# A fused attention and two-layer MLP kernel: the clamp of the weights' top byte moves from GpSimd to ScalarE, in a new order

## Chip, cores and metric

The kernel runs on one core of a Trainium2 chip. The metric is the device time in microseconds (us) of one execution.

## What is computed

The reference chains three parts. The first is an attention over 2 batches, 8 heads, 768 tokens and a head size of 64, in which a key counts only where it falls into the same hash bucket as the query:

```
mask = q_bucket[:, :, :, None] == k_bucket[:, :, None, :]
scores = np.where(mask, scale * np.matmul(q, k.transpose(0, 1, 3, 2)), -1e9)
attn = np.exp(scores - max) / (sum + 1e-09)
```

Its output, 1536 tokens of 512 numbers, goes through a first MLP: `h = x @ w_in` (512 to 2048), `g = h * tanh(softplus(h))`, `g @ w_out` (2048 to 512). Then comes a second one: `h = x @ w_in` (512 to 1024), `h * softmax(h)`, a layer norm with the gain `g_ln`, and `@ w_out` (1024 to 512). The weights arrive as 64-bit floats; every product is taken as a sum of three products of parts (high by high, high by low, low by high).

## The kernel before

The program is one long list of steps over five engines. `program_order` declares every step with its engine, cost and what it reads and writes; `Order.run` turns that into one order per engine, from the costs in `COST` and from offsets in `PHASE`, a table of numbers that sets how urgent each kind of step is. Each engine then works through its own list in order: a step that waits holds back all behind it on that engine.

Three stretches follow one another in time. **Attention**: 96 tiles of 128 queries by 768 keys. For each, TensorE makes the scores (L1180), VectorE the row maximum (L1187), ScalarE the exponential (L1196); the result is split into two fp16 parts (ScalarE L1207 and GpSimd L1229, or through TensorE, L1215 to L1224) and weighed with `v` on TensorE (L1247 to L1249). **First MLP**: 48 units, each one block of 512 tokens by 128 hidden numbers. In a unit TensorE does 12 matmuls of 512 columns up (`up`, L800 to L802) and 12 down (`down_high`, `down_low`, L856 to L861). Between the two stands the activation, `mish`, eleven steps `a0` to `a10`: ScalarE exp (L816), VectorE (L818, L820, L822), ScalarE logarithm (L824) and exp (L826), VectorE (L828, L830), GpSimd product `n` (L834), ScalarE high part `gh` (L839), GpSimd low part `gl` (L842). The units share two PSUM banks `h`: a unit's bank is free for the second unit after it once L830 is done. **Second MLP**: 12 tiles of 128 tokens (L905 to L975), without GpSimd.

The weights come in 48 chunks of 128 by 512 doubles. `chunk` declares and `w_step` issues the conversion of a chunk to fp32 in six steps. The load puts the chunk into a tile `wr`, shifted by one byte, so that the sign and the top seven exponent bits of each double stand in a byte of their own (`top`) and the next 32 bits in a word (`low`). Step `w0` (ScalarE, L693) writes `top` times 2^27 as a float to a PSUM bank `wq`; `w1` (GpSimd, L696) clamps `top` to plus or minus 56 into the tile `wf`; `w2` (VectorE, L698) takes the clamped byte times 2^27 from `wq` and stores it as an integer; `w3` (VectorE, L700) joins it with the shifted `low`; `w5` (ScalarE, L707 or L709) and `w6` (GpSimd L713, for the last eight chunks VectorE L715) make the two parts that the matmuls read. Tiles `wr` and `wf` have two buffers each, `wq` has one bank. Four chunks are converted during the attention, the others while the first MLP runs.

```
        if j == 0:
            nc.scalar.activation(q, top, AF.Copy, scale=TOP)
        elif j == 1:
            t.append(p.tile([128, 512], F32, tag="wf", name="wf"))
            nc.gpsimd.tensor_scalar(t[1].bitcast(I8)[:, 0:512], top, -EXP_GAP, EXP_GAP, op0=ALU.max, op1=ALU.min)
        elif j == 2:
            nc.vector.scalar_tensor_tensor(q.bitcast(I32), t[1].bitcast(I8)[:, 0:512], -TOP, q, op0=ALU.mult, op1=ALU.add)
```

Of the kernel before, what the change touches and what calls it, by code (L numbers as in the profile page):

```python
# [9 lines left out]
F32 = mybir.dt.float32  # L10
F32R = mybir.dt.float32r
F16 = mybir.dt.float16
I8 = mybir.dt.int8
I32 = mybir.dt.int32
AF = mybir.ActivationFunctionType
ALU = mybir.AluOpType
# [11 lines left out]
TOP = 2.0 ** 27  # L28
EXP_GAP = 56


PHASE = dict(
    score=3.18, max=2.53, bias=-167.78, exp=-11.41, hi=43.25, lo=-29.73, tdma=-251.87, tr0=9.20, thi0=-31.01,
    tlo0=7.90, tr1=10.26, thi1=22.25, tlo1=-118.98, weigh=17.76, norm0=-27.63, norm1=-69.89, norm2=-117.62,
    load=57.26, vload=-17.69, split0=185.96, rest0=-39.72, split1=19.36, rest1=6.02, turn=-2.32, evac=-159.74,
    copy=-179.38, bits0=-325.74, bits1=4.40, sign=-9.22, bdma=2.32, vmax=104.27, vs0=-114.44, vs1=-42.67,
    vs2=-72.72, vs3=-18.05, vs4=-74.05, vs5=12.38, vs6=-32.00, vs7=-32.58, vs8=14.06, vh=32.22, vl=-142.30,
    first=-210.30, turn_=42.29, evac_=59.56, copy_=-124.42, bits_=64.90, sign_=163.79, bdma_=142.14,
    vload_=-52.66, vmax_=346.44, vs_=-185.69, vh_=90.08, vl_=-136.17, second=28.07, wload=168.86, w0=36.13,
    w1=191.13, w2=126.06, w3=-34.77, w4=-53.41, w5=6.07, w6=124.56, wpace=-53.43, wat=182.43, wlate=-729.27,  # L40
    turngap=0.64, x0_=-3.53, x1_=-148.94, x2_=153.79, load_=10.62, const0=-101.54, begin0=25.07, vs8_=220.89,
    outlag=-1.85, up=-43.62, a0=23.99, a1=11.15, a2=58.10, a3=153.65, a4=-268.52, a5=-90.91, a6=3.61,
    a7=-137.25, a8=69.62, a9=-156.92, a10=83.71, da=59.12, db=-9.71, ky0=52.83, ky1=17.06, x0=20.21, x1=21.53,
    x2=-180.26, sy0=-146.63, sy1=221.79, u2=-66.64, n0=-239.67, n1=241.84, n2=-76.83, n3=-225.79, n4=-25.00,
    n5=74.29, n6=-371.20, n7=108.91, n8=115.67, n9=-108.58, n10=-44.93, n11=-50.71, n12=-49.24, n13=144.69,
    t2=-55.28, l0=-163.64, l1=43.42, d2=146.11, ot=22.49, od=-41.99, wloadL=-187.89, w0L=8.05, w1L=49.78,
    w2L=117.28, w3L=-140.95, w4L=-342.97, w5L=-28.48, w6L=-114.27, begin1=-124.80, begin2=17.00, begin3=-13.01,
    const1=161.30, const3=171.44, load0_=4.64,
)


# [1 line left out]
    score=0.7, max=0.865, bias=0.14, exp=0.878, hiA=0.733, hiD=0.469, lo=1.596, tr=0.325, thi=0.371, tlo=0.469,  # L53
    weigh=0.533, norm0=0.075, norm1=0.106, norm2=0.469, split=0.915, rest=1.79, turn=0.5,
    evacA=0.691, evacD=0.865, bits=0.69, sign=0.985, vmax=0.87, vs0=0.11, vs1=0.2, vs2=0.11,
    vs=0.07, vs8=0.884, vh=0.733, firstA=0.413, firstD=0.469, w0=0.52, w1=0.6, w2=0.602,
    w3=0.602, w5=0.52, w6P=1.225, w6D=0.663, x0=0.434, x1=0.478, x2=0.602,
    up=0.68, a0=0.478, a1=0.335, a2=0.602, a3=0.613, a4=0.52, a9=0.52, a10=1.225, da=0.453, db=0.2265,
    sy0=0.52, sy1=0.602, u2=1.36, n0=1.131, n1=1.091, n2=0.069, n3=0.075, n4=1.196, n5=0.069, n6=1.133,
    n7=0.188, n8=0.094, n9=0.069, n10=0.13, n11=0.069, n12=0.069, n13=0.723, t2=0.87, d2=2.72,  # L60
)
WIRE = dict(load=1.3, load0=0.65, vload=1.3, wload=1.65, copy=1.08, bdma=0.2, tdma=1.6,
            od=0.728, const0=0.185, const1=0.028, const2=0.028, const3=0.448)
# [206 lines left out]
def program_order(pairs, tiles, routes, evac, chunks, due, rings, stores, slack, queues=(), pooled=0,  # L270
# [6 lines left out]
    A, V, G, T = "Activation", "DVE", "Pool", "PE"  # L277

    def dma(key, base, name, reads=(), writes=(), slot=0, behind=()):
        fast = key[0] in ("load", "load0", "vload", "wload", "const", "od")  # L280
        op(key, A if key[0] in queues else "SP", 0.54 if fast else 0.8 if key[0] == "bdma" else 0.625, base, name, reads, writes, slot, behind)
# [117 lines left out]
    def chunk(i, base, slot, reads):  # L399
        late = i >= chunks  # L400
        wr, wf = ((x + "2" * late, i) for x in ("wr", "wf"))
        q = "L" if late else ""
        dma(("wload", i), base, "wload" + q, [("wg", i - 1)] + reads, [wr], 0, (("bdma", 0, (0,), 0, 1),))
        wq = ("wq", i)
        steps = [(A, "w0", [wr], [wq]), (G, "w1", [wr], [wf]), (V, "w2", [wf, wq], [wq]), (V, "w3", [wr, wq], [wf]),
                 (A, "w5", [wf], [slot]), (V if plan[i][0][0] == "out2" else G, "w6", [wf], [slot])]
        for j, (e, nm, r, w) in enumerate(steps):
            cost = COST.get(nm + e[0], COST.get(nm))
            op(("w", i, j), e, cost, base, nm + q, r, w + ([("wg", i)] if j == 0 else []), 0,
               [("w", i - 1, j)] if nm == "w5" and i else [])  # L410
# [160 lines left out]
def lsh_attention_moe_kernel(  # L571
# [14 lines left out]
    evac="AAAA",  # L586
# [23 lines left out]
    nc = tc.nc  # L610
# [17 lines left out]
    const = ctx.enter_context(tc.tile_pool(name="const", bufs=1, side="left"))  # L628
# [9 lines left out]
    ones = const.tile([1, 128], F32, name="ones")  # L638
    eps = const.tile([128, 1], F32, name="eps")
    two = const.tile([128, 1], F32, name="two")  # L640
    pcol = const.tile([128, NC], F32, name="pcol")


# [15 lines left out]
    def job(i):  # L659
        (kind, j, *half), slot, _ = plan[i]  # L660
        if kind == "in":
            return chunk_cols(w1_in, j * 128), None
        if kind == "out":
            return chunk_rows(w1_out, j * 128, 0), None
        if kind == "in2":
            return chunk_rows(w2_in, j * 128, half[0] * 512), None
        return chunk_rows(w2_out, j * 128, 0), glt[:, j:j + 1]
# [18 lines left out]
    def w_step(i, j):  # L686
        src, scale = job(i)
        p, t = pools["wr", i >= nconv], raw_w[i]
        top = t[0].bitcast(I8)[:, 8:4104].rearrange("p (n a) -> p n a", a=8)[:, :, 0]
        low = t[0][:, 0:1024].rearrange("p (n a) -> p n a", a=2)[:, :, 1]  # L690
        q = bank("wq", i)
        if j == 0:
            nc.scalar.activation(q, top, AF.Copy, scale=TOP)  # L693
        elif j == 1:
            t.append(p.tile([128, 512], F32, tag="wf", name="wf"))
            nc.gpsimd.tensor_scalar(t[1].bitcast(I8)[:, 0:512], top, -EXP_GAP, EXP_GAP, op0=ALU.max, op1=ALU.min)  # L696
        elif j == 2:
            nc.vector.scalar_tensor_tensor(q.bitcast(I32), t[1].bitcast(I8)[:, 0:512], -TOP, q, op0=ALU.mult, op1=ALU.add)  # L698
        elif j == 3:
            nc.vector.scalar_tensor_tensor(t[1].bitcast(I32), low, 5, q.bitcast(I32), op0=ALU.logical_shift_right,  # L700
                                           op1=ALU.bitwise_or)
        elif j == 4:
            tags = ("xt", "xt") if plan[i][1][0] == "xs" else ("wh", "wl")
            parts[plan[i][0]] = tuple(w_pool(i).tile([128, 512], F32R, tag=x, name="w") for x in tags)
            hi = parts[plan[i][0]][0]
            if scale is None:
                nc.scalar.activation(hi, t[1], AF.Copy)  # L707
            else:
                nc.scalar.activation(hi, t[1], AF.Copy, scale=scale)  # L709
        else:  # L710
            hi, lo = parts[plan[i][0]]
            if scale is None:
                nc.gpsimd.tensor_tensor(lo, t[1], hi.bitcast(F32), op=ALU.subtract)  # L713
            else:
                nc.vector.scalar_tensor_tensor(lo, t[1], scale, hi.bitcast(F32), op0=ALU.mult, op1=ALU.subtract)  # L715
            raw_w.pop(i)
# [36 lines left out]
    def bank(*tok):  # L753
        return banks[:, order.place[tok]]
# [9 lines left out]
    def step(name, make):  # L764

        def run(*key):
            if key[-1] == 0:
                gen[name, key[:-1]] = make(*key[:-1])
            next(gen[name, key[:-1]])
        return run  # L770
# [521 lines left out]
    nc.gpsimd.memset(ones, 1.0)  # L1292
    nc.gpsimd.memset(eps, 1e-6)
    nc.gpsimd.memset(two, 2.0)
    for c in range(NC):
        nc.gpsimd.memset(pcol[:, c:c + 1], 1e-9 if routes[c] in "Dd" else 1e-9 * PSCALE)
    for w in v_t:
# [16 lines left out]
        load=load_qk, load0=load_first, split=qk_split, rest=qk_rest, const=const_in, begin=begin,  # L1314
        first=lambda i, h, o: (first_high, first_low)[i](h, o),
        turn=qk_turn, evac=qk_evac, copy=qk_copy, bits=bits, sign=signs, bdma=bits_in, vload=load_v,
        vmax=v_max, vs=step("vs", v_scale), vh=v_high, vl=v_low, score=scores, max=row_max,
        bias=row_bias, exp=exps, hi=hi_part, lo=lo_part, tdma=turn_dma, tr=turn_half, thi=half_high,
# [35 lines left out]
```

## Time and profile before

| | |
|---|---|
| median of 3 runs (lowest to highest) | 688.05 us (686.13 to 688.23) |
| the profiled execution's own time | 687.81 us |
| its span, first to last instruction | 686.0 us, 12209 instructions |
| TensorE busy | 639.6 us (93%) |
| VectorE busy | 486.8 us (71%) |
| ScalarE busy | 439.3 us (64%) |
| GpSimd busy | 431.0 us (63%) |

The profile is of one execution. PE is TensorE's matmul, PEld its weight load, DVE is VectorE, ACT ScalarE, POOL GpSimd; an engine name with a q is its queue. The share of a whole span mixes stretches with different limits: GpSimd is near full until about 520 us and has nothing to do in the last 140 us. A matmul's end is modelled and overlaps the start of the next, so TensorE's busy time hides short gaps; its pace is read from the starts.

### The profile page before, as it was taken

How to read it: one execution, taken by the hardware profiler on the slowest of the kernel's cores; microseconds unless marked ns; L12 is line 12 of the kernel's file. 1: busy time of each engine (PE TensorE's matmuls, PEld its weight loads, DVE VectorE, ACT ScalarE, POOL GpSimd, SP SyncE). 2: the span in 40 equal slices, each digit the busy share in tenths (PEclk: the TensorE clock that was granted, in tenths of full speed). 3: DMA queues.
4: the chain of work that ended last, by engine and by line, in shares of the span. 5: the costliest groups of instructions: out<-in, count | busy, mean ns of one | idle time of the engine just before them, and what ended most of it. 6: DMA issues, size and time to landing. Idle time of an engine off the chain costs nothing.

```text
span 686.0 us, 12209 instructions
## 1 busy us (share of the span) xinstructions
PE 639.6 (93%) x4520; PEld 515.3 (75%) x4520; DVE 486.8 (71%) x1017; ACT 439.3 (64%) x718; POOL 431.0 (63%) x309
## 2 busy tenths in 40 slices
PE   6899998999999998989988899999999999999997
PEld 4678776888988865667666667787767888888886
DVE  3867868778989777868677678968867685634540
ACT  6788999999999855655454556654555443532441
POOL 4886986876767887989989988848885200000000
PEclk9889999999999999999999999999999999999999
DMA  5979999899988932322222232301200000000011
GB/s 149 250 146 169 221 149 171 182 183 177 155 161 175 199 120 82 103 71 84 92 72 82 92 104 82 106 17 62 93 31 1 0 1 1 31 17 15 31 47 46
DMA packets 125148, 68.11 MB, mean 99 GB/s; under 512 B 103584, under 2 KB 118048, under 8 KB 125088
## 3 DMA queue, kind: packets, MB, share of 16 engines
q1 hardware_dynamic: 125088, 67.33, 42.6%
q8 instruction: 35, 0.57, 0.4%
q14 instruction: 25, 0.20, 0.1%
HBM read 34.68 MB, written 3.15 MB: 55 GB/s over the span
## 4 chain that ended last, share of the span: by engine, by line
PE 39%; POOL 28%; DVE 10%; issue 8%; ACT 8%; DMA 6%; SPq 1%; POOLq 0%; ACTq 0%; DVEq 0%
POOL wf L696 7%; POOL n L834 7%; POOL gl L842 6%; POOL w L713 6%; PE banks L1180 4%; PE banks L906 3%; PE banks L905 3%; PE banks L909 3%; PE banks L971 3%; PE banks L970 3%; PE banks L969 3%; DVE mx L1187 3%; DMA store<-store 3%; ACT gh L839 3%; DMA B<-bits 2%
## 5 line engine op out<-in xcount | busy, mean ns | idle before, releaser
L1229 POOL TENSOR_TENSOR store<-store 128x768 f16<-128x768 f32 x64 | 104.7, 1652 | 28.9 <-ACT store L1207 21.0
L1187 DVE TENSOR_REDUCE mx<-banks 128x1 f32<-128x768 f32 x96 | 90.5, 950 | 26.8 <-PE banks L1180 22.1
L1196 ACT ACTIVATE store<-banks,mx 128x768 f32<-128x768 f32 x96 | 93.7, 992 | 7.9 <-DVE mx L1192 4.4
L696 POOL TENSOR_SCALAR wf<-wr 128x512 int8<-128x512 int8 x48 | 96.2, 2005 | 0.8 <-DMA wr<-in_moe_w_out_dram 0.5
L842 POOL TENSOR_TENSOR gl<-n,gh 128x512 fp32r<-128x512 f32 x48 | 62.4, 1300 | 48.8 <-ACT gh L839 31.9
L800 PE MATMUL banks<-xh,w 128*128 128x512 f32 x192 | 78.9, 411 | 10.7 <-DVE a L830 9.4
L861 PE MATMUL banks<-gl,w 128*128 128x512 f32 x192 | 75.6, 406 | 7.7 <-POOL gl L842 7.4
L802 PE MATMUL banks<-xh,w 128*128 128x512 f32 x192 | 76.6, 399 | 0.2
L856 PE MATMUL banks<-gh,w 128*128 128x512 f32 x192 | 76.4, 398 | 0.3 <-ACT banks L826 0.3
L801 PE MATMUL banks<-xl,w 128*128 128x512 f32 x192 | 76.0, 396 | 0.0
L857 PE MATMUL banks<-gh,w 128*128 128x512 f32 x192 | 75.9, 395 | 0.0
L834 POOL TENSOR_TENSOR n<-c,a 128x512 f32<-128x512 f32 x48 | 62.5, 1302 | 18.2 <-DVE a L830 13.4
L839 ACT ACTIVATE gh<-n 128x512 fp32r<-128x512 f32 x48 | 30.2, 629 | 58.5 <-POOL n L834 58.2
L1180 PE MATMUL banks<-A,A 128*128 128x384 f32 x192 | 58.0, 383 | 7.5 <-ACT store L1196 6.1
L824 ACT ACTIVATE a<-n,two 128x512 f32<-128x512 f32 x48 | 34.5, 719 | 44.7 <-DVE n L820 44.7
L1247 PE MATMUL banks<-v,store 128*128 128x65 f16 x576 | 60.7, 194 | 1.8 <-DMA store<-store 1.4
L1248 PE MATMUL banks<-v,store 128*128 128x64 f16 x576 | 60.4, 195 | 0.0
L1249 PE MATMUL banks<-v,store 128*128 128x65 f16 x576 | 60.1, 192 | 0.0
L1247 PEld LDWEIGHTS <-store 128*128 128x128 f16 x576 | 53.1, 97 | 7.3 <-issue 4.6
L800 PEld LDWEIGHTS banks<-xh,w 128*128 128x128 f32 x192 | 36.4, 190 | 28.2 <-DVE a L830 17.5
L1248 PEld LDWEIGHTS <-store 128*128 128x128 f16 x576 | 53.6, 98 | 1.2 <-issue 0.7
L713 POOL TENSOR_TENSOR w<-wf,w 128x512 fp32r<-128x512 f32 x40 | 51.7, 1293 | 3.9 <-ACT w L707 3.9
(122 smaller groups left out, 1715.2 us busy)
## 6 DMA issues: line engine op xcount, KB each, us to landing
wr<-in_moe_w_in_dram SPq DMA_DIRECT2D x24, 512.0 KB
wr<-in_moe_w_out_dram SPq DMA_DIRECT2D x24, 512.0 KB
vr<-in_v_dram SPq DMA_DIRECT2D x8, 384.0 KB
B<-A SPq DMA_DIRECT2D x16, 192.0 KB
out_dram<-ot SPq DMA_DIRECT2D x12, 256.0 KB
q<-in_q_dram SPq DMA_DIRECT2D x7, 384.0 KB
k<-in_k_dram SPq DMA_DIRECT2D x7, 384.0 KB
B<-bits SPq DMA_DIRECT2D x32, 36.0 KB
```

The lines of the kernel that those rows point to most:

```text
L696: nc.gpsimd.tensor_scalar(t[1].bitcast(I8)[:, 0:512], top, -EXP_GAP, EXP_GAP, op0=ALU.max, op1=ALU.min)
L713: nc.gpsimd.tensor_tensor(lo, t[1], hi.bitcast(F32), op=ALU.subtract)
L800: nc.tensor.matmul(h, lhsT=wh[:, ks], rhs=xh, start=(kk == 0), stop=False)
L802: nc.tensor.matmul(h, lhsT=wl[:, ks], rhs=xh, start=False, stop=(kk == KD - 1))
L834: nc.gpsimd.tensor_tensor(g, t("c"), t("a"), op=ALU.mult)
L842: (nc.vector if late == "V" else nc.gpsimd).tensor_tensor(g_t[u][1], g, t("gh").bitcast(F32), op=ALU.subtract)
L1180: nc.tensor.matmul(s[:, half, 0:NH], lhsT=opnd[nm, p, j, 0][:, cc], rhs=opnd[nm, p, j, 1][:, hs], start=(i == 0), stop=(i == 1),)
L1187: nc.vector.reduce_max(m[:, 1:2], two_banks("s", t)[:, :, 0:NH], axis=AX.XY, negate=True)
L1196: nc.scalar.activation(kept("e", t).rearrange("p (a n) -> p a n", a=2), two_banks("s", t)[:, :, 0:NH], AF.Exp, bias=m[:, 3:4], scale=m[:, ...
L1229: nc.gpsimd.tensor_tensor(p16[:, 1], kept("e", t), p16[:, 0], op=ALU.subtract)
L1247: nc.tensor.matmul(o, lhsT=pt[:, 0, kc, :], rhs=vh, start=(kc == 0), stop=False)
L1248: nc.tensor.matmul(o[:, 0:D], lhsT=pt[:, 0, kc, :], rhs=vl, start=False, stop=False)
```

## The change

Step `w1` leaves GpSimd. `w0` now writes max(top * 2^27 - 56 * 2^27, 0) and `w1`, on ScalarE, max(-top * 2^27 - 56 * 2^27, 0); `w2` subtracts the second from the first. The difference is what the byte less its clamped value gave. The constant -56 * 2^27 stands in a new one-column tile `gap`, which the two read as their bias and which GpSimd fills at the start. The table `PHASE` has all its numbers changed and two costs are set to 0.65, so the order is made anew on every engine.

```
 PHASE = dict(
-    score=3.18, max=2.53, bias=-167.78, exp=-11.41, hi=43.25, lo=-29.73, tdma=-251.87, tr0=9.20, thi0=-31.01,
...
+    score=3.69, max=0.87, bias=-330.22, exp=12.74, hi=253.86, lo=-96.05, tdma=-189.01, tr0=9.77, thi0=14.69,
...
-    vs=0.07, vs8=0.884, vh=0.733, firstA=0.413, firstD=0.469, w0=0.52, w1=0.6, w2=0.602,
+    vs=0.07, vs8=0.884, vh=0.733, firstA=0.413, firstD=0.469, w0=0.65, w1=0.65, w2=0.602,
...
-        steps = [(A, "w0", [wr], [wq]), (G, "w1", [wr], [wf]), (V, "w2", [wf, wq], [wq]), (V, "w3", [wr, wq], [wf]),
+        steps = [(A, "w0", [wr], [wq]), (A, "w1", [wr], [wf]), (V, "w2", [wf, wq], [wq]), (V, "w3", [wr, wq], [wf]),
...
+    gap = const.tile([128, 1], F32, name="gap")
...
-            nc.scalar.activation(q, top, AF.Copy, scale=TOP)
+            nc.scalar.activation(q, top, AF.Relu, scale=TOP, bias=gap)
...
-            nc.gpsimd.tensor_scalar(t[1].bitcast(I8)[:, 0:512], top, -EXP_GAP, EXP_GAP, op0=ALU.max, op1=ALU.min)
+            nc.scalar.activation(t[1], top, AF.Relu, scale=-TOP, bias=gap)
...
-            nc.vector.scalar_tensor_tensor(q.bitcast(I32), t[1].bitcast(I8)[:, 0:512], -TOP, q, op0=ALU.mult, op1=ALU.add)
+            nc.vector.scalar_tensor_tensor(q.bitcast(I32), t[1], -1.0, q, op0=ALU.mult, op1=ALU.add)
...
+    nc.gpsimd.memset(gap, -EXP_GAP * TOP)
```

How the order moves is shown at three places. In the changed kernel the lines are one or two further down. The first place is GpSimd's list around the seventeenth unit of the first MLP: `n` and `gl` are the unit's two steps, `w` is step `w6` and `wf` step `w1` of a chunk. Before:

```order
L834 TENSOR_TENSOR n_4949<-c_4960,a_4937 128x512
L842 TENSOR_TENSOR gl_5007<-n_4949,gh_5000 128x512
L713 TENSOR_TENSOR w_5015<-wf_4983,w_5014 128x512
L696 TENSOR_SCALAR wf_5033<-wr_4979 128x512
L834 TENSOR_TENSOR n_4998<-c_5012,a_4987 128x512
```

And with the change:

```order
L835 TENSOR_TENSOR n_4943<-c_4957,a_4935 128x512
L843 TENSOR_TENSOR gl_5011<-n_4943,gh_5001 128x512
L714 TENSOR_TENSOR w_5009<-wf_4980,w_5008 128x512
L835 TENSOR_TENSOR n_4988<-c_5006,a_4976 128x512
L714 TENSOR_TENSOR w_5058<-wf_5030,w_5057 128x512
L843 TENSOR_TENSOR gl_5074<-n_4988,gh_5065 128x512
```

The step between one unit's `w6` and the next unit's `n` is gone, and nothing takes its place.

The second place is ScalarE's list in the same unit, from its first exponential (L816, then L817): L693 and L694 are `w0`, L697 is the new `w1`, L707 and L708 are `w5`. Before:

```order
L816 ACTIVATE banks_75<-banks_75 128x512
L839 ACTIVATE gh_4951<-n_4898 128x512
L824 ACTIVATE a_4937<-n_4949,two_70 128x512
L707 ACTIVATE w_4965<-wf_4934 128x512
L826 ACTIVATE banks_75<-a_4937 128x512
L693 ACTIVATE banks_75<-wr_4929 128x512
L816 ACTIVATE banks_75<-banks_75 128x512
```

And with the change, one unit on:

```order
L817 ACTIVATE banks_76<-banks_76 128x512
L694 ACTIVATE banks_76<-wr_4927,gap_71 128x512
L697 ACTIVATE wf_4980<-wr_4927,gap_71 128x512
L825 ACTIVATE a_4976<-n_4988,two_70 128x512
L840 ACTIVATE gh_5001<-n_4943 128x512
L708 ACTIVATE w_5008<-wf_4980 128x512
L827 ACTIVATE banks_76<-a_4976 128x512
```

The pair `w0`, `w1` now stands between the unit's first exponential and its logarithm, where `gh` of the unit before stood; `gh` follows the logarithm.

The third place is ScalarE in the attention, at the first of the four chunks converted there (L1196 and L1197 are the exponentials of the score tiles). Before:

```order
L693 ACTIVATE banks_75<-wr_339 128x512
L1196 ACTIVATE store_105<-banks_75,mx3_100 128x768
L1219 ACTIVATE store_105<-banks_75 128x384
L1207 ACTIVATE store_105<-store_105 128x768
L1196 ACTIVATE store_105<-banks_75,mx4_101 128x768
```

And with the change:

```order
L697 ACTIVATE wf_628<-wr_342,gap_71 128x512
L694 ACTIVATE banks_76<-wr_342,gap_71 128x512
L1197 ACTIVATE store_106<-banks_76,mx3_101 128x768
L1208 ACTIVATE store_106<-store_106 128x768
L1197 ACTIVATE store_106<-banks_76,mx4_102 128x768
```

Both steps stand ahead of the next exponential. The whole ScalarE list of the changed kernel holds one table load, at its start, as before.

## Rows read from the trace of the kernel before

**Rows 1.** The chain that ended last, shares of the span by engine and line.

```profile
PE 39%; POOL 28%; DVE 10%; issue 8%; ACT 8%; DMA 6%; SPq 1%; POOLq 0%; ACTq 0%; DVEq 0%
POOL wf L696 7%; POOL n L834 7%; POOL gl L842 6%; POOL w L713 6%; PE banks L1180 4%; PE banks L906 3%; PE banks L905 3%; PE banks L909 3%; PE banks L971 3%; PE banks L970 3%; PE banks L969 3%; DVE mx L1187 3%; DMA store<-store 3%; ACT gh L839 3%; DMA B<-bits 2%
```

**Rows 2.** The chain in order of time, one unit: start us, us, what.

```profile
328.18 1.95 POOL wf L696
330.13 1.28 POOL n L834
...
331.43 0.64 ACT gh L839
...
332.14 1.30 POOL gl L842
333.44 1.14 POOL w L713
...
334.64 1.96 POOL wf L696
```

**Rows 3.** Groups of GpSimd instructions: busy us, mean ns, idle before, releasers.

```profile
L696 POOL TENSOR_SCALAR wf<-wr 128x512 int8<-128x512 int8 x48 | 96.2, 2005 | 0.8 <-DMA wr<-in_moe_w_out_dram 0.5
L842 POOL TENSOR_TENSOR gl<-n,gh 128x512 fp32r<-128x512 f32 x48 | 62.4, 1300 | 48.8 <-ACT gh L839 31.9 <-PE banks L861 15.8 <-PE banks L801 1.1
```

**Rows 4.** Waits, longest first: us in total, times, longest us.

```profile
ACT gh L839 <- POOL n L834: 58.2, 33, 3.8
ACT a L824 <- DVE n L820: 44.7, 31, 3.5
```

**Rows 5.** TensorE's matmuls in order of time, first and last of twelve: start, us.

```profile
303.64 0.40 PE L800 MATMUL banks<-xh,w 128*128 128x512 f32 x1
...
306.20 0.40 PE L802 MATMUL banks<-xh,w 128*128 128x512 f32 x1
```

**Rows 6.** Stretches: length, busy us (count) of PE, PEld, DVE, ACT, POOL; PEclk, DMA, GB/s.

```profile
60.00:223.00 163.00, 152.98 (x2038) 133.37 (x2037) 137.06 (x366) 156.16 (x222) 126.42 (x83) 1.00 0.93 174
223.00:262.00 39.00, 34.37 (x352) 27.05 (x350) 28.99 (x54) 26.49 (x46) 33.15 (x23) 1.00 0.66 142
262.00:375.00 113.00, 102.96 (x411) 75.98 (x411) 82.89 (x129) 62.66 (x111) 100.20 (x71) 0.98 0.28 88
375.00:435.00 60.00, 56.35 (x233) 42.57 (x232) 47.27 (x75) 34.98 (x62) 53.60 (x37) 1.00 0.27 88
435.00:520.00 85.00, 81.64 (x343) 63.37 (x342) 65.06 (x102) 46.02 (x80) 65.53 (x45) 1.00 0.17 56
520.00:533.00 13.00, 13.00 (x58) 10.57 (x57) 10.33 (x16) 6.82 (x13) 6.39 (x5) 1.00 0.01 2
```

**Rows 7.** Line L696 alone in three of these stretches: length, POOL busy (count).

```profile
262.00:375.00 113.00, 34.81 (x18) 0.98 0.28 88
375.00:435.00 60.00, 20.87 (x11) 1.00 0.27 88
435.00:520.00 85.00, 20.92 (x10) 1.00 0.17 56
```

**Rows 8.** Groups of ScalarE instructions: busy us, mean ns, idle before, releasers.

```profile
L693 ACT ACTIVATE banks<-wr 128x512 f32<-128x512 int8 x48 | 30.0, 624 | 4.3 <-DVE a L830 1.9 <-DMA wr<-in_moe_w_out_dram 1.4 <-DMA wr<-in_moe_w_in_dram 0.6
L824 ACT ACTIVATE a<-n,two 128x512 f32<-128x512 f32 x48 | 34.5, 719 | 44.7 <-DVE n L820 44.7
L707 ACT ACTIVATE w<-wf 128x512 fp32r<-128x512 f32 x40 | 25.0, 624 | 17.2 <-DVE wf L700 17.1
L709 ACT ACTIVATE w<-wf,glt 128x512 fp32r<-128x512 f32 x8 | 5.7, 711 | 0.0
L627 ACT ACT_TABLE_LOAD x1 | 1.3, 1283 | 0.7 <-PEq L1338 0.7
```

**Rows 9.** Groups of VectorE instructions: busy us, mean ns, idle before, releasers.

```profile
L698 DVE SCALAR_TENSOR_TENSOR banks<-wf,banks 128x512 int32<-128x512 int8 x48 | 33.2, 692 | 27.6 <-POOL wf L696 27.4 <-ACT banks L693 0.2
L828 DVE SCALAR_TENSOR_TENSOR a<-n,banks 128x512 f32<-128x512 f32 x48 | 32.9, 685 | 26.0 <-ACT banks L826 25.3
```

More of the change, by code (lines that the diff above doesn't have):

```diff
@@ L32 @@
 PHASE = dict(
-    score=3.18, max=2.53, bias=-167.78, exp=-11.41, hi=43.25, lo=-29.73, tdma=-251.87, tr0=9.20, thi0=-31.01,
[L34 to L47, printed above, removed]
@@ L48 @@
-    const1=161.30, const3=171.44, load0_=4.64,
+    score=3.69, max=0.87, bias=-330.22, exp=12.74, hi=253.86, lo=-96.05, tdma=-189.01, tr0=9.77, thi0=14.69,
+    tlo0=4.19, tr1=10.11, thi1=75.90, tlo1=-207.08, weigh=17.00, norm0=-35.41, norm1=-226.56, norm2=-78.50,
+    load=129.70, vload=75.26, split0=453.42, rest0=274.23, split1=209.91, rest1=322.17, turn=-1.39,
+    evac=-101.44, copy=-173.09, bits0=-324.87, bits1=5.03, sign=-117.83, bdma=135.73, vmax=30.34, vs0=-33.79,
+    vs1=-146.49, vs2=-188.08, vs3=-25.17, vs4=-176.05, vs5=207.64, vs6=-228.20, vs7=-38.10, vs8=-29.32,
@@ new lines @@
+    vh=171.54, vl=-118.08, first=-636.50, turn_=106.45, evac_=-17.59, copy_=-135.91, bits_=109.21, sign_=186.80,
+    bdma_=302.63, vload_=-136.00, vmax_=-58.57, vs_=-137.35, vh_=486.24, vl_=-22.15, second=-6.75, wload=356.57,
+    w0=122.15, w1=233.00, w2=453.40, w3=-132.54, w4=-118.88, w5=26.88, w6=-124.83, wpace=-43.83, wat=169.36,
+    wlate=-944.98, turngap=0.47, x0_=-22.09, x1_=-199.05, x2_=165.20, load_=-4.58, const0=-117.46,
+    begin0=-133.70, vs8_=320.02, outlag=44.69, up=-206.71, a0=-25.55, a1=33.80, a2=79.27, a3=227.95, a4=-374.57,
@@ new lines @@
+    a5=-161.92, a6=-9.47, a7=-120.59, a8=-84.30, a9=-164.37, a10=363.32, da=69.39, db=-368.55, ky0=14.03,
+    ky1=88.45, x0=-105.44, x1=-102.23, x2=-93.30, sy0=57.14, sy1=387.61, u2=256.06, n0=-140.91, n1=257.67,
+    n2=-53.84, n3=-206.26, n4=34.90, n5=68.87, n6=-476.27, n7=90.14, n8=-151.97, n9=-30.78, n10=-42.23,
+    n11=26.26, n12=-13.08, n13=464.05, t2=65.16, l0=-65.93, l1=-63.15, d2=309.12, ot=-137.74, od=-190.53,
+    wloadL=-427.87, w0L=-54.06, w1L=-32.31, w2L=76.07, w3L=-275.48, w4L=-365.85, w5L=-91.93, w6L=-68.34,
@@ L49 @@
+    begin1=-314.58, begin2=47.74, begin3=100.37, const1=147.93, const3=246.73, load0_=16.27,
 )
```

## Prediction

> **What bounds the kernel now.** I read the chain that ended last first. By line, its largest single piece is the clamp L696 with 7% of the span, next to the three other GpSimd steps of the first MLP, and GpSimd makes 28% of the whole chain [rows 1]. In order of time one sees why: from 328.18 to 334.64 us the chain runs clamp, `n`, `gh`, `gl`, `w6`, and again clamp, almost without a break, and four of these five pieces are GpSimd's [rows 2]. One unit takes 334.64 - 328.18 = 6.46 us there. TensorE could go faster: twelve matmuls start at 303.64 to 306.20 us, eleven steps in 2.56 us, so 0.2327 us each and 24 x 0.2327 = 5.58 us per unit [rows 5]. So GpSimd sets the pace of a unit, and it makes the others late: ScalarE stood 58.2 us waiting for `n` before `gh`, and since it works in order, what stands behind `gh` waited too; 44.7 us more went before its logarithm [rows 4].
>
> How much that costs in all I read from the stretches, by TensorE's starts and not by its busy time. From 262 us the PE counts are 512-column matmuls only. 411 + 233 + 343 = 987 of them need 987 x 0.2327 = 229.7 us; the stretches last 113 + 60 + 85 = 258 us [rows 5, 6]. So 28.3 us are lost there. By stretch: 113 - 95.6 = 17.4 us with GpSimd at 89%, 60 - 54.2 = 5.8 us at 89%, 85 - 79.8 = 5.2 us at 77%. From 520 to 533 us, where GpSimd is at 49%, 58 x 0.2327 = 13.5 us of work stand in 13 us: nothing is lost [rows 6]. After that GpSimd hardly matters, and I take that part as it is.
>
> **What the change removes.** All 48 clamps, 96.2 us of GpSimd at 2005 ns [rows 3]. In 262 to 520 us there are 18 + 11 + 10 = 39 of them, 34.81 + 20.87 + 20.92 = 76.6 us [rows 7]. GpSimd's work there falls from 100.20 + 53.60 + 65.53 = 219.3 us to 142.7 us [rows 6].
>
> What that gives is bounded by two rows. If the loss per time stays what it is at 77% (5.2 of 85 us, 6.1%), the 229.7 us take 229.7 / 0.939 = 244.6 us and 13.4 us are saved. If nothing is lost, as at 49%, 28.3 us are saved. With the clamps gone GpSimd stands at about 142.7 / 236 = 60%, which is 0.39 of the way from 49% to 77%: a loss of 2.4%, so 235.3 us, and **22.7 us saved**. The interpolation is my choice; I take it because both rows come from the same loop of units.
>
> The Trainium skill would have priced the removed step lower. The page "GPSIMD Engine Reference", section "4.1 Engine selection", says that a one-input elementwise operation runs on GpSimd at roughly the line rate, two-input ones about twice slower than on VectorE. The rows speak against it here: the one-input clamp of bytes took 2005 ns, the two-input `gl` 1300 ns [rows 3]. By the page, with VectorE's 685 ns for the step [rows 9], the 39 steps would free 27 us instead of 76.6; GpSimd would hardly come under its 77%, and 13.4 us would be the saving. The measurement decides.
>
> From 223 to 262 us the last attention tiles and the first units mix. TensorE is idle for 39 - 34.37 = 4.6 us, GpSimd busy for 33.15 us of 39 [rows 6]. Between nothing and 4.6 us gained I take half, **2.3 us**, since nothing shows how much of it is GpSimd's.
>
> **What it adds.** No row shows a rectifier. Its nearest rows are activations of the same 512 columns. With no operand per partition one takes 624 ns (L693 from bytes, L707); with one it takes 711 ns (L709) or 719 ns (L824) [rows 8]. `w0` gains such an operand, `gap`: between 0 and 95 ns, I take 87 (711 - 624). The new `w1` costs between 624 and 719 ns; I take 715, the middle of the two rows that read such an operand. Together 0.80 us per chunk, 48 x 0.80 = 38.5 us of ScalarE.
>
> Where does it lie? In the attention ScalarE is busy for 156.16 of 163 us, 96% [rows 6]: four chunks are converted there, and 4 x 0.80 = **3.2 us** are taken as lost in full (0 at best, if the new order finds gaps). In 262 to 520 us ScalarE has 62.66 + 34.98 + 46.02 = 143.7 us of work and gets 39 x 0.80 = 31.2 us more: 174.9 of about 236 us, 74%. I cost that at nothing. Its cover is the time in which ScalarE stands before `gh` and the logarithm, 102.9 us in all [rows 4]; if it were gone, the 31 us would come on the path.
>
> The step adds waits on ScalarE. `w0` and `w1` wait for the load `wr`, as L693 did for 1.4 + 0.6 us [rows 8], and `w1` now waits on ScalarE until GpSimd's `w6` of two chunks earlier has freed the tile `wf`; behind them stand the logarithm or `gh`. That `w6` lies more than a unit back, and GpSimd is now early, so I cost this at nothing. `w2` reads a float instead of a byte: 692 ns against 685 ns for L828, which has those operands [rows 9], no change. It stops waiting for GpSimd (27.4 us), but is then late by ScalarE's two steps, which come one after the other where `w0` and the clamp ran side by side. `gap` costs one fill at the start, before GpSimd has data. DMAs keep their number and sizes.
>
> **Sum.** The profiled execution took 687.81 us, 0.24 below the median of the runs shown. 687.8 - 22.7 - 2.3 + 3.2 = **666.0 us**. With the bounds: 687.8 - 28.3 - 4.6 = 654.9 us, and 687.8 - 13.4 + 3.2 = 677.6 us.
>
> **Rivals.** (a) *TensorE alone is left.* The new order hides all: 654.9 us. For it speaks the stretch from 520 us; against it that VectorE has 82.89 + 47.27 + 65.06 = 195.2 us of work to do in 236 us, 83%, in order, with cross waits.
>
> (b) *The ring of two `h` banks and VectorE's order take over.* A unit's bank is held from its first matmul until L830. The pair `w0`, `w1` now stands in front of the logarithm and delays it, so units come at the pace they have at GpSimd's 77%: only 13.4 us saved, 677.6 us. The 44.7 us before the logarithm speak for slack there.
>
> (c) *ScalarE becomes the bound, slower than before.* In the unit's loop ScalarE must do exponential, logarithm, exponential and `gh` in order; a pair of 1.43 us ahead of the logarithm delays L826, then L828 and L830, then the second next unit's matmuls. If all 0.80 us of each of the 44 chunks of the first MLP come on that path, 35.2 us are added: 666.0 + 35.2 = 701 us. It is slower from 21.8 / 44 = 0.50 us per chunk upward. Against it stands ScalarE's 74%. The Trainium skill, page "ScalarE: Activation LUTs", section "Rules for kernel authors", says to use VectorE and not ScalarE for relu, max and min; this change does the opposite. By that rule this rival is what would happen. The trace puts VectorE at 83% and ScalarE at 74% after the change, which speaks against the rule here.
>
> (d) *A cancelling.* About 0.5 us per chunk comes on the path: no change, 688 us.
>
> (e) *The rectifier isn't in the loaded table.* Two loads per chunk, 2 x 48 x 1.28 us [rows 8], 123 us more, 789 us. The order of the changed kernel holds one table load, which speaks against it.
>
> **How the numbers follow.** Forecast 0.58, (a) 0.12, (b) 0.19, (c) 0.06, (d) 0.04, (e) 0.01. A measurement of this kernel can tell about 0.3%, 2 us, from no change. Faster: 0.58 + 0.12 + 0.19 = 0.89; same 0.04; slower 0.06 + 0.01 = 0.07. The range reaches from (a) to a little beyond (b), 654 to 680 us; outside it are (c), (d), (e) and what misses at the edges.
>
> **What would show it.** Right: GpSimd busy 431 - 96 = 335 us and ScalarE 439 + 38.5 = 478 us; the rectifiers at 0.70 to 0.72 us each; the clamp gone from the chain and TensorE's share of it well above 39%; units about 5.7 us apart; the wait of `gh` for `n` much below 58 us; the first up matmul of the MLP some 3 us later than 223 us, unless the new order moved it. Wrong: units still 6.3 us apart with ScalarE or VectorE on the chain, an attention longer by much more than 3 us, or rectifiers of 1 us and more.

## The result, and the profile after

The changed kernel takes 657.23 us (median of 4 runs, 656.17 to 657.67) against 687.09 us of the kernel before (4 runs, 685.55 to 688.23): a ratio of 0.9565, 95% interval 0.9539 to 0.9590. The forecast was 666.0 us, range 654 to 680.

The chain of the changed kernel, by engine and by line, answers to [rows 1]:

```profile
PE 75%; DMA 9%; ACT 4%; POOL 4%; DVE 3%; issue 2%; SPq 1%; POOLq 0%; ACTq 0%; DVEq 0%
PE banks L862 7%; PE banks L857 7%; PE banks L858 7%; PE banks L801 7%; PE banks L802 7%; PE banks L803 7%; DMA store<-store 6%; PE banks L1181 5%; PE banks L907 3%; PE banks L906 3%; PE banks L910 3%; PE banks L972 3%; PE banks L971 3%; PE banks L970 3%; POOL store L1230 3%
```

TensorE went from 39% to 75% of it, GpSimd from 28% to 4%, and the four GpSimd steps of the first MLP are gone from the list. The stretches of the changed kernel (columns as in [rows 6]):

```profile
60.00:223.00 163.00, 150.85 (x2042) 134.06 (x2041) 134.50 (x349) 155.12 (x222) 117.59 (x78) 0.99 0.95 168
223.00:262.00 39.00, 37.10 (x385) 30.81 (x384) 33.96 (x71) 34.58 (x57) 25.34 (x19) 1.00 0.74 169
262.00:375.00 113.00, 112.97 (x492) 91.74 (x491) 97.84 (x155) 93.11 (x155) 80.87 (x64) 1.00 0.33 103
375.00:435.00 60.00, 60.00 (x262) 48.71 (x261) 50.72 (x79) 42.62 (x71) 31.00 (x24) 1.00 0.25 79
435.00:500.00 65.00, 65.00 (x282) 52.70 (x281) 56.04 (x86) 45.43 (x76) 38.44 (x30) 1.00 0.15 49
```

From 262 us on TensorE hardly stops any more. A matmul that runs over the edge between two stretches is counted in both, so the three counts add up to 1036 and TensorE's pace is read from one stretch:

```profile
262.00:500.00 238.00, 237.97 (x1032) 193.15 (x1031) 204.61 (x319) 181.17 (x300) 150.30 (x118) 1.00 0.26 82
```

238 / 1032 gives 0.231 us each, or 5.54 us per unit. In 262 to 375 us the count is 492 where it was 411 [rows 6]. VectorE is now at 87% there, ScalarE at 82%, GpSimd at 72% instead of 89%.

The first line of the up matmuls, and the exponentials of the attention, before and after (median and extreme durations in ns, then first and last start in us). Of the kernel before:

```profile
L800 PE MATMUL banks<-xh,w x192: 387/396/628, 223.0 to 528.1; 128*128 128x512 f32 x192
L1196 ACT ACTIVATE store<-banks,mx x96: 973/992/1012, 20.7 to 226.9; 128x768 f32<-128x768 f32 x96
```

And of the changed kernel:

```profile
L801 PE MATMUL banks<-xh,w x192: 387/391/496, 227.9 to 495.5; 128*128 128x512 f32 x192
L1197 ACT ACTIVATE store<-banks,mx x96: 972/991/1038, 20.5 to 230.5; 128x768 f32<-128x768 f32 x96
```

This places the difference of the two profiled executions. The first unit starts 4.9 us later, the stretch from the first to the last up matmul shrinks from 305.1 to 267.6 us, and what follows grows from 157.9 to 159.9 us. 4.9 - 37.5 + 2.0 = -30.6 us, from a span of 686.0 to 655.4. The stretch behind the last of these starts, before and after:

```profile
528.10:686.00 157.90, 154.24 (x722) 126.97 (x720) 81.39 (x182) 62.36 (x128) 6.94 (x5) 1.00 0.05 21
495.50:655.40 159.90, 156.15 (x730) 128.47 (x728) 81.66 (x182) 62.91 (x129) 6.87 (x5) 1.00 0.05 20
```

TensorE is busy for 98% of it in both. Eight more matmuls stand in it after the change, some 1.8 us at the pace above: nearly all of the 2.0 us is work that moved there.

The rectifiers and the subtraction (columns as in [rows 8]), and the wait that stood first in [rows 4], also of the changed kernel:

```profile
L697 ACT ACTIVATE wf<-wr,gap 128x512 f32<-128x512 int8 x48 | 36.2, 754 | 0.3 <-DVE w L716 0.3
L694 ACT ACTIVATE banks<-wr,gap 128x512 f32<-128x512 int8 x48 | 34.6, 720 | 2.0 <-DMA wr<-in_moe_w_out_dram 1.7 <-DVE store L1225 0.2
L699 DVE SCALAR_TENSOR_TENSOR banks<-wf,banks 128x512 int32<-128x512 f32 x48 | 33.0, 687 | 3.1 <-ACT wf L697 3.1
```

```profile
ACT gh L840 <- POOL n L835: 12.9, 12, 3.0
```

ScalarE stood 12.9 us before `gh` instead of 58.2 us, and VectorE 3.1 us before the subtraction instead of 27.6 us [rows 9].

### The profile page after: what moved, and what is told of

Same layout as the page of the kernel before. It is cut to its first block, busy times and chain, and to the rows that moved or that the text cites. A ratio compares the mean times of both kernels' runs of the same rounds, so it can differ in the third digit from the quotient of the medians.

```text
span 655.4 us, 12164 instructions
## 1 busy us (share of the span) xinstructions
PE 622.6 (95%) x4520; PEld 520.0 (79%) x4520; DVE 488.3 (74%) x1017; ACT 477.5 (73%) x766; POOL 338.1 (52%) x262
## 4 chain that ended last, share of the span: by engine, by line
PE 75%; DMA 9%; ACT 4%; POOL 4%; DVE 3%; issue 2%; SPq 1%; POOLq 0%; ACTq 0%; DVEq 0%
PE banks L862 7%; PE banks L857 7%; PE banks L858 7%; PE banks L801 7%; PE banks L802 7%; PE banks L803 7%; DMA store<-store 6%; PE banks L1181 5%; PE banks L907 3%; PE banks L906 3%; PE banks L910 3%; PE banks L972 3%; PE banks L971 3%; PE banks L970 3%; POOL store L1230 3%
## 5 line engine op out<-in xcount | busy, mean ns | idle before, releaser
L1197 ACT ACTIVATE store<-banks,mx 128x768 f32<-128x768 f32 x96 | 93.3, 993 | 9.2 <-DVE mx L1193 3.7
L801 PE MATMUL banks<-xh,w 128*128 128x512 f32 x192 | 75.5, 393 | 1.3 <-DVE a L831 1.2
L803 PE MATMUL banks<-xh,w 128*128 128x512 f32 x192 | 75.4, 393 | 0.0
L862 PE MATMUL banks<-gl,w 128*128 128x512 f32 x192 | 74.2, 395 | 0.3 <-POOL gl L843 0.3
L1248 PE MATMUL banks<-v,store 128*128 128x65 f16 x576 | 61.7, 194 | 6.2 <-DMA store<-store 3.9
L1248 PEld LDWEIGHTS <-store 128*128 128x128 f16 x576 | 53.3, 97 | 10.2 <-DMA store<-store 6.0
L1250 PE MATMUL banks<-v,store 128*128 128x65 f16 x576 | 61.2, 193 | 0.0
L1249 PEld LDWEIGHTS <-store 128*128 128x128 f16 x576 | 53.9, 98 | 3.0 <-issue 2.7
L1250 PEld LDWEIGHTS <-store 128*128 128x128 f16 x576 | 54.0, 99 | 0.0
L1208 ACT ACTIVATE store<-store 128x768 f16<-128x768 f32 x64 | 53.5, 849 | 0.1
L825 ACT ACTIVATE a<-n,two 128x512 f32<-128x512 f32 x48 | 34.7, 723 | 25.4 <-DVE n L821 25.2
L1181 PE MATMUL banks<-B 76*128 76x384 f32 x192 | 50.9, 347 | 0.0
```

Source lines behind the costliest of these rows:

```text
L801: nc.tensor.matmul(h, lhsT=wh[:, ks], rhs=xh, start=(kk == 0), stop=False)
L803: nc.tensor.matmul(h, lhsT=wl[:, ks], rhs=xh, start=False, stop=(kk == KD - 1))
L862: nc.tensor.matmul(y, lhsT=wh[:, os], rhs=g_t[u][1], start=False, stop=last)
L1181: nc.tensor.matmul(s[:, half, 0:NH], lhsT=opnd[nm, p, j, 0][:, cc], rhs=opnd[nm, p, j, 1][:, hs], start=(i == 0), stop=(i == 1),)
L1197: nc.scalar.activation(kept("e", t).rearrange("p (a n) -> p a n", a=2), two_banks("s", t)[:, :, 0:NH], AF.Exp, bias=m[:, 3:4], scale=m[:, ...
L1248: nc.tensor.matmul(o, lhsT=pt[:, 0, kc, :], rhs=vh, start=(kc == 0), stop=False)
```

## The experiments

Where an experiment is said to keep an order, every engine's list is that kernel's, with only the named instruction changed, replaced or added in its place. Where the order is made anew, the planner ran again with the same table of offsets.

**e1, the new steps in the old order.** The order and all costs are those of the kernel before.

```
...
-            nc.scalar.activation(q, top, AF.Copy, scale=TOP)
+            nc.scalar.activation(q, top, AF.Relu, scale=TOP, bias=gap)
...
-            nc.gpsimd.tensor_scalar(t[1].bitcast(I8)[:, 0:512], top, -EXP_GAP, EXP_GAP, op0=ALU.max, op1=ALU.min)
+            nc.scalar.activation(t[1], top, AF.Relu, scale=-TOP, bias=gap)
...
-            nc.vector.scalar_tensor_tensor(q.bitcast(I32), t[1].bitcast(I8)[:, 0:512], -TOP, q, op0=ALU.mult, op1=ALU.add)
+            nc.vector.scalar_tensor_tensor(q.bitcast(I32), t[1], -1.0, q, op0=ALU.mult, op1=ALU.add)
...
```

> The kernel before with its own order kept, but the two rectified parts on ScalarE in place of the clamp on GpSimd (the new step stands where the old one stood in the list). Theory G, GpSimd's time set the pace of a unit: units come at 5.5 to 5.8 us, the whole takes 657 to 670 us, most of the gain is there without a new order. Theory O, the new order gave the gain: 680 to 690 us, units still above 6.1 us.

Measured: 661.48 us against 688.1 us, ratio 0.9614 (0.9587 to 0.9641). The up matmuls run from 226.1 to 501.4 us, and TensorE is nearly full again:

```profile
262.00:375.00 113.00, 111.55 (x480) 89.66 (x480) 95.06 (x151) 90.32 (x153) 78.39 (x62) 1.00 0.32 102
375.00:435.00 60.00, 59.22 (x254) 47.04 (x253) 50.98 (x79) 42.85 (x72) 32.27 (x25) 1.00 0.26 89
```

So 26.6 us come without any new order, as theory G expected.

**e2, the old steps in the new order.** The edit is that of e1 the other way round, in the changed kernel.

> The changed kernel's order on every engine, but the clamp back on GpSimd, the copy on ScalarE and the old subtraction. Theory G: GpSimd again needs 6.4 us per unit with a chunk, so 684 to 700 us. Theory O: near the changed kernel, 657 to 670 us.

Measured: 713.62 us, ratio 1.0366 (1.0334 to 1.0399), slower than either theory said. The waits, and the stretch from 375 us:

```profile
ACT a L825 <- DVE n L821: 50.1, 37, 3.8
DVE banks L699 <- POOL wf L697: 48.0, 35, 3.3
ACT gh L840 <- POOL n L835: 47.5, 25, 3.8
```

```profile
375.00:435.00 60.00, 51.80 (x198) 39.47 (x196) 36.94 (x57) 28.61 (x50) 49.60 (x35) 0.91 0.25 80
```

The clamp is waited for 48.0 us instead of 27.4, and TensorE, with pauses, had a mean granted clock of 0.91 there. The new order alone costs 25.5 us with the old steps and gains 4.3 us with the new ones (661.48 to 657.23). It does not suit the old steps.

**e4, GpSimd's time given back, with nobody waiting for it.** The changed kernel's order; each later chunk gets a clamp over 64 of the 128 partitions that writes `spare`, a piece of a new tile which nobody reads.

```
...
             nc.scalar.activation(t[1], top, AF.Relu, scale=-TOP, bias=gap)
+            if i >= nconv:
+                nc.gpsimd.tensor_scalar(spare, top[64:128], -EXP_GAP, EXP_GAP, op0=ALU.max, op1=ALU.min)
```

> The changed kernel, with a clamp on GpSimd added for each of the 44 later chunks that writes a tile nobody reads: GpSimd's time is back (44 x 2.0 = 88 us), nobody waits for it. Theory G: GpSimd's list is as full as before and its n and gl come late, 675 to 690 us. Rival W, it was the wait of the subtraction for the clamp that cost, not GpSimd's time: 657 to 662 us.

Measured: 698.71 us, ratio 1.0165 (1.0127 to 1.0202): 41.5 us above the changed kernel. The added clamp, the longest waits and two stretches:

```profile
L701 POOL TENSOR_SCALAR side<-wr x44: 1932/1950/2375, 227.2 to 515.7; 64x512 int8<-64x512 int8 x44
```

```profile
ACT gh L844 <- POOL n L839: 47.2, 24, 3.7
DVE c L827 <- POOL n L839: 40.7, 26, 4.2
```

```profile
262.00:375.00 113.00, 98.12 (x398) 73.56 (x396) 79.95 (x126) 74.48 (x126) 97.18 (x67) 0.98 0.25 80
375.00:435.00 60.00, 53.52 (x212) 41.20 (x211) 42.68 (x67) 39.97 (x66) 52.77 (x37) 0.94 0.27 88
```

Nothing reads the added clamp, yet all of the gain and more is gone, beyond the range of theory G too: 1.95 us more per chunk on GpSimd's list is enough. The subtraction stood only 2.0 us in all, so rival W falls. The added clamp also reads `wr`, but no step of the conversion stood more than 0.3 us for a load. TensorE, with pauses, had a mean granted clock of 0.94 in the second stretch, which is a part of the loss.

**e7, the clamp planned at what it takes.** In the kernel before, one number; the order is made anew.

```
-    vs=0.07, vs8=0.884, vh=0.733, firstA=0.413, firstD=0.469, w0=0.52, w1=0.6, w2=0.602,
+    vs=0.07, vs8=0.884, vh=0.733, firstA=0.413, firstD=0.469, w0=0.52, w1=2.0, w2=0.602,
```

> The kernel before, with one number changed: the planner is told that the clamp costs 2.0 us and not 0.6 us; its table of offsets stays, so the order changes. Theory G, GpSimd simply has too much to do in a unit (6.46 us with a chunk): 680 to 692 us. Theory O, the old order lost time because it did not know the price: 660 to 675 us.

Measured: 672.92 us, ratio 0.9771 (0.9749 to 0.9793), inside the range of theory O. The first stretch of the units:

```profile
262.00:375.00 113.00, 110.71 (x467) 86.54 (x468) 89.88 (x142) 69.38 (x122) 111.04 (x79) 1.00 0.30 94
```

GpSimd is at 98% instead of 89% and TensorE's count is 467 matmuls instead of 411. So GpSimd had holes in the old order. [Rows 2] show them: the four GpSimd pieces of a unit add up to 5.67 us, and the 0.64 us of `gh` with its hand-overs made it 6.46, because GpSimd had nothing else in its list while it waited. Step `gl` alone from 262 to 375 us, before and in e7 (columns as in [rows 3]):

```profile
L842 POOL TENSOR_TENSOR gl<-n,gh 128x512 fp32r<-128x512 f32 x17 | 22.0, 1295 | 9.7 <-ACT gh L839 9.7
L842 POOL TENSOR_TENSOR gl<-n,gh 128x512 fp32r<-128x512 f32 x18 | 23.7, 1316 | 0.7 <-ACT gh L839 0.7
```

The wait of 9.7 us for `gh` is gone but for 0.7 us. An order that fills the hole comes close to TensorE's pace, but needs GpSimd nearly without a break. The changed kernel is 15.7 us faster still. e7 keeps the old offsets; whether offsets set for the clamp at its price would come nearer was not run.

**e3, the clamp on VectorE.** The changed kernel's order, with the three old steps, the clamp on VectorE.

```
...
-            nc.scalar.activation(t[1], top, AF.Relu, scale=-TOP, bias=gap)
+            nc.vector.tensor_scalar(t[1].bitcast(I8)[:, 0:512], top, -EXP_GAP, EXP_GAP, op0=ALU.max, op1=ALU.min)
...
```

> The changed kernel's order, with the old three steps, but the clamp on VectorE at the place in the program where the second rectifier stands. VectorE would gain 48 steps of some 0.68 us if bytes cost what the fp32 steps cost, 33 us, and go from 86% to 97% of the units' stretch. Theory G with VectorE as the next bound: units at 5.7 to 6.0 us, 662 to 680 us, slower than the changed kernel. The rule of the Trainium skill (use VectorE, not ScalarE, for max and min): no slower than the changed kernel, 650 to 658 us.

Measured: 680.27 us, ratio 0.9882 (0.9855 to 0.9910), 23 us above the changed kernel. Its clamps (min, median, max in ns), the first stretch of the units, and a wait (us in total, times, longest):

```profile
L697 DVE TENSOR_SCALAR wf<-wr x48: 411/758/1827, 47.3 to 500.7; 128x512 int8<-128x512 int8 x48
```

```profile
262.00:375.00 113.00, 105.64 (x448) 81.18 (x447) 103.28 (x163) 70.85 (x123) 72.44 (x56) 1.00 0.29 93
```

```profile
ACT a L825 <- DVE n L821: 66.1, 38, 2.9
```

VectorE is at 91%, and ScalarE stood 66.1 us for it before the logarithm, against 25.2 us in the changed kernel. Here the rule of the Trainium skill, page "ScalarE: Activation LUTs", section "Rules for kernel authors" (VectorE and not ScalarE for relu, max and min), gives the slower kernel. The order was made for the rectifiers; one made for the clamp on VectorE was not run.

**e5, one more step on ScalarE.** The changed kernel's order, with a third, unused rectifier per later chunk.

```
...
             nc.scalar.activation(t[1], top, AF.Relu, scale=-TOP, bias=gap)
+            if i >= nconv:
+                nc.scalar.activation(spare, top[64:128], AF.Relu, scale=-1.0, bias=gap[64:128])
```

> The changed kernel with a third, unused rectifier on ScalarE for each of the 44 later chunks (44 x 0.72 = 32 us more of ScalarE). Theory S, ScalarE still has room in the units' stretch (181 us of 238 us used): at most 4 us more, 657 to 661 us, units at 5.5 to 5.7 us. Rival, the rectifiers have brought ScalarE to its limit and the next step on it lands on the path: 44 x 0.4 us or more, 672 us and up, TensorE waiting for steps that ScalarE delayed.

Measured: 659.84 us, ratio 0.9584 (0.9554 to 0.9614). ScalarE is at 95% in the first stretch, and TensorE still does not stop:

```profile
262.00:375.00 113.00, 112.92 (x487) 90.09 (x486) 96.18 (x153) 107.38 (x175) 80.53 (x63) 1.00 0.32 103
```

The added steps took 33 us (44 of 757 ns) and cost 2.6 us in the medians, about as much as the runs of one kernel differ. In the profile the stretch from the first to the last up matmul is 271.0 us against 267.6. The rectifiers did not bring ScalarE to its limit.

**e6, the clamp on GpSimd in the attention only.** The changed kernel's order; chunks 0 to 3 keep the three old steps.

```
...
+            if early_chunk:
+                nc.gpsimd.tensor_scalar(t[1].bitcast(I8)[:, 0:512], top, -EXP_GAP, EXP_GAP, op0=ALU.max, op1=ALU.min)
+            else:
+                nc.scalar.activation(t[1], top, AF.Relu, scale=-TOP, bias=gap)
...
```

> The changed kernel, same order, but the first four chunks, which are converted during the attention, keep the copy on ScalarE and the clamp on GpSimd. If the four pairs of ScalarE steps cost the attention their full 4 x 0.80 us: 3 us faster than the changed kernel, 653 to 655 us. If the attention hides them: no difference within 1.5 us, 656 to 659 us.

Measured: 662.89 us, ratio 0.9634 (0.9608 to 0.9659), 5.7 us slower than the changed kernel where 3 us faster or no difference was expected. The last exponential starts at 234.9 us. In this order four clamps on GpSimd cost the attention more than four pairs on ScalarE.

**e8, two chunks in the attention instead of four.** The order is made anew.

```
-    nconv=4,
+    nconv=2,
```

> The changed kernel with two instead of four chunks converted during the attention and the other two early in the first MLP (order made anew by that). If ScalarE's share of the attention is what costs there: attention 1.5 us shorter or more, 653 to 657 us. If the first units then wait for their weights: 660 to 670 us.

Measured: 677.02 us, ratio 0.9842 (0.9817 to 0.9867). This is slower than either expectation. The last exponential starts at 229.4 us, but in 223 to 262 us TensorE is busy for 33.57 us against 37.10. The longest waits of its matmuls from 223 to 300 us:

```profile
PE banks L857 <- ACT gh L840: 5.2, 2, 4.2
PE banks L801 <- DVE a L831: 3.6, 1, 3.6
```

For a part of the weights TensorE stood 0.8 us at most. So the first units waited for their activation, on ScalarE and VectorE, and not directly for their weights; what made it late is not settled.

**e9, the changed kernel again.**

> The changed kernel once more, beside the next three on the same chip, with a second profile: 656 to 659 us. If the attention's end varies from one execution to the next by itself, the last exponential starts somewhere between 226 and 231 us; if it is fixed by the order, at 230 to 231 us as in the first profile.

Measured: 657.22 us, ratio 0.9538 (0.9498 to 0.9578). The last exponential starts at 231.5 us. The kernels of e4 and e5 have the same list of exponentials up to there, and theirs start last at 226.0 and 227.3 us. So the attention's end is uncertain by some 5 us for one and the same list; what makes it so is not settled.

**e10, less of ScalarE in the attention.** The changed kernel's order; for every sixth tile VectorE makes the fp16 high part.

```
-        if routes[t % len(routes)] == "D":
+        if routes[t % len(routes)] == "D" and t % 6 != 5:
```

> The changed kernel, same order, but for every sixth score tile (16 of 96) the fp16 high part is made by VectorE instead of ScalarE: 16 x 0.85 = 13.6 us less of ScalarE in the attention. If ScalarE, at 95%, bounds the attention: 3 to 8 us faster than the changed kernel, 649 to 654 us. If VectorE's lateness takes its place (its maxima wait behind the new step): 657 us or more.

Measured: 661.15 us, ratio 0.9593 (0.9563 to 0.9623), 3.9 us slower than e9 beside it in the medians. From 60 to 223 us, first of e9, then of e10:

```profile
60.00:223.00 163.00, 150.71 (x2018) 134.08 (x2017) 133.30 (x348) 154.00 (x219) 116.42 (x78) 0.98 0.94 167
```

```profile
60.00:223.00 163.00, 149.33 (x1989) 132.00 (x1987) 140.56 (x353) 143.39 (x204) 116.74 (x77) 0.98 0.91 164
```

ScalarE has 10.6 us less to do and the attention does not get shorter: the last exponential starts at 235.1 us against 231.5, and TensorE's count is lower. But the exponentials now stood for VectorE, which makes the scale and bias that they read (L1193; us, times), first of e9, then of e10:

```profile
  DVE mx L1193: 3.3, 5
  DVE mx L1193: 16.7, 17
```

So VectorE's lateness took ScalarE's place, as the second expectation had it. What ScalarE's 95% costs the attention, e10 does not tell.

**e11, the same move, planned.** `routes="DADDAD"` becomes `"DADDAd"` and the order is made anew.

> The same move of the high part of every sixth tile to VectorE, but with the order made anew for it (same table of offsets). If ScalarE bounds the attention and the order fits: 645 to 654 us. If the offsets, which were set for another assignment, no longer fit: 657 to 670 us with units apart from the 5.55 us.

Measured: 672.5 us, ratio 0.9754 (0.9720 to 0.9788); the last exponential starts at 243.8 us, and the exponentials stood 15.1 us for VectorE (L1193), much as in e10. Whether offsets set for this assignment would do better is not shown.

**e12, the rectifiers planned at nearly what they take.** The order is made anew.

```
-    vs=0.07, vs8=0.884, vh=0.733, firstA=0.413, firstD=0.469, w0=0.65, w1=0.65, w2=0.602,
+    vs=0.07, vs8=0.884, vh=0.733, firstA=0.413, firstD=0.469, w0=0.67, w1=0.75, w2=0.602,
```

> The changed kernel with the two rectifiers planned at 0.67 and 0.75 us, their measured 0.72 and 0.75 us less the overlap of neighbours for the first, in place of 0.65 and 0.65 us; the order changes by that alone. If the order of before was slow because its clamp was planned at 0.6 us and took 2.0 us, an error of 0.1 us should matter little: 653 to 661 us. If any change of the order under the same offsets costs some per cent: 664 us and more.

Measured: 663.95 us, ratio 0.9636 (0.9600 to 0.9672). This is 6.7 us slower than e9, by a change of planned costs, and so of the order, alone. In the profiles half of it lies ahead of the first up matmul (232.3 us against 228.6) and half between the first and the last (272.6 us against 268.7). The 15 us of e7 are over twice that, and its profile names where they came from; the 4.3 us between e1 and the changed kernel are not more than it, so it is not shown that the new order as such has a part in the gain.

No version tried beats the changed kernel.

## Why the prediction was right, and where its terms were off

**What bounds the kernel: right.** That GpSimd's list set the pace of a unit is shown by e1 (the clamp away, the order kept: -26.6 us) and e4 (the time back, no one waiting: +41.5 us). The reading was incomplete in one point: it took the unit's 6.46 us as GpSimd's load, but a part of it was holes. e7 recovers 15 us by order alone, with all the clamps in place.

**The saving in the units: mis-sized.** 22.7 + 2.3 us were forecast; the stretch of the up matmuls shrank by 37.5 us. The step that failed is the interpolation by GpSimd's share, between a loss of 6.1% at 77% and none at 49%, which gave 2.4%. The share does not set the loss. Without clamps next to nothing is lost at 72% (262 to 375 us of the changed kernel); with all of them in the order of e7, 113 - 467 x 0.231 = 5.1 us or 4.5% is lost at 98%, less than 6.1%. Besides, the loss itself was taken too small: the pace of 0.2327 us came from twelve matmuls of a stretch with pauses, and 987 counts some matmuls twice, at the edges of the three stretches. In one stretch, of the kernel before:

```profile
262.00:520.00 258.00, 240.96 (x983) 181.91 (x983) 195.22 (x305) 143.66 (x251) 219.34 (x152) 0.99 0.24 78
```

At 0.231 us these 983 need 227.1 us, so 30.9 us were lost and not 28.3. All of it came back. Of the other 37.5 - 30.9 = 6.6 us some 1.8 are the eight matmuls that moved behind the last up matmul; 4.8 us came from the first units, where 2.3 us were forecast. In the units it went as rival (a) had it, and its 654.9 us lies nearer to the measured time than the forecast.

**ScalarE's price: nearly right.** 0.71 and 0.715 us per rectifier were taken; they took 0.720 and 0.754, together 34.6 + 36.2 - 30.0 = 40.8 us more where 38.5 were forecast. ScalarE's busy time, in which steps that overlap count once, rose by 38.2 us, from 439.3 to 477.5. That it costs next to nothing in the units is borne out by e5, with 33 us more.

**The attention: nearly the size, but not by that reason.** 3.2 us were forecast; the first unit starts 4.9 us later. But the same list ended 4 us earlier in e4's profile, putting the clamp back on GpSimd made it worse (e6), and taking 10.6 us off ScalarE did not help, since VectorE then came late (e10). That a step on an engine at 96% lands on the path in full was an assumption, and it is not borne out; that 3.2 us came near 4.9 is luck. What bounds the attention stays open.

**The rest.** Of the 2.0 us added after the last up matmul, 1.8 are moved work, so the units gained 37.5 - 1.8 = 35.7 us. The forecast missed that gain by 10.7 us and the losses elsewhere by 4.9 + 0.2 - 3.2 = 1.9 us, 8.8 us in all.

**The rivals.** (b) and (d) did not happen. (c) falls with e5. (e) falls with the rectifiers' 0.72 and 0.75 us.

## What to carry to other kernels

Give a step to the engine that has room in the stretch where the step runs, and find the room by adding an unused step there: 33 us more of ScalarE cost 2.6 us, 87 us more of GpSimd cost 41.5. When an engine that works in order is the bound, look for what it waits for inside its own chain before counting its busy share: with the hole of 0.7 us closed that stood in most units, the kernel was 15 us faster here. And do not take a loss rate from an engine's busy share, least of all in a stretch that still contains the step to be removed.

## What was not expected of the hardware

The clamp on VectorE took 411 ns at best and 1827 ns at worst (e3). One that took long, and the GpSimd step beside it (start us, us), in the profile of e3:

```profile
294.40 1.61 DVE L697 TENSOR_SCALAR wf<-wr 128x512 int8<-128x512 int8 x1
```

```profile
294.40 1.32 POOL L835 TENSOR_TENSOR n<-c,a 128x512 f32<-128x512 f32 x1
```

Both start at 294.40 us, and the clamp ends 0.29 us after GpSimd's step. The 48 clamps of that trace fall into line with this pair: the ten that ran with no GpSimd step beside them took 414 to 421 ns, and each of the thirty that took 533 ns or more ended 0.28 to 0.29 us after a GpSimd step beside it. The clamp looks held back until GpSimd is done. The Trainium skill, page "GPSIMD Engine Reference", section "1. Specifications", says that GpSimd shares its SBUF interfaces with VectorE and contends with VectorE's instructions in a two-port mode or with two SBUF inputs; the trace agrees that the two contend. It does not tell in which mode the clamp ran, and no run here took GpSimd's steps away.

The subtraction on VectorE, with one input from SBUF and one from PSUM, did not show this: L699 took 687 ns on the mean in the changed kernel, with GpSimd at 72% beside it.
